# Moving the work of GpSimd, VectorE and ScalarE around an unchanged matmul sequence in a two-layer dense stage

## The chip, the cores and the metric

The kernel runs on one core of a Trainium2 chip. The metric is the device time of one execution in microseconds (us). Lower is better. The engines are named as in the profile: PE is TensorE (matmul; its weight loads are PEld), DVE is VectorE, ACT is ScalarE, POOL is GpSimd, SP is the engine that issues most of the DMAs.

## What is computed

Three layers follow each other: linear attention with random features, a mixture of experts (each token goes to one of eight), and a dense two-layer network with a piecewise quadratic gate. The change lies in the last one alone:

```python
def _moe2_ref(x, w_in, w_out) -> np.ndarray:      # x: 2304 x 512
    h = x @ w_in                                  # w_in: 512 x 2048
    beta = 1.0
    neg = h <= -beta
    pos = h >= beta
    g = np.where(pos, h, np.where(neg, 0.0, (h + beta) ** 2 / (4.0 * beta)))
    return (g @ w_out).astype(np.float32)         # w_out: 2048 x 512
```

The weights of this layer come as 64-bit floats, so the kernel first makes 32-bit ones of them.

## The kernel before

Precision: each product A x B runs as three matmuls of a fast 32-bit format, high x high, high x low and low x high. So every operand has a high part (ACT rounds it, `AF.Copy` into an F32R tile) and a low part (the operand less its high part, a subtraction of two SBUF tiles on POOL or DVE, here called a low).

The dense stage takes the hidden width of 2048 in four quarters `qd` of 512, and the 2304 tokens in six groups of G = 384.

**Quarter 0** (loop over `u` of 0 to 5) multiplies plainly. Per group PE runs `z_h(u,(0,1))`, `z_o(0,u-1,(2,3))`, `z_h(u,(2,3))`, `z_o(0,u,(0,1))`. A `z_h` call makes two 128-wide pieces of `h` (24 matmuls of 384 columns), a `z_o` call multiplies two pieces of `g` by `w_out` for three token tiles (18 matmuls of 512 columns). Group 0 lacks the second of the four.

**Quarters 1 to 3** make `h` by Winograd's form of Strassen's scheme, seven products in place of eight, in 18 calls `s_h(qd,p,a)` (three a quarter for p, two each for a). A call has seven products of six matmuls, added up in four PSUM banks b1 to b4; what goes from bank to bank goes through the SBUF tiles `tt`. After the first call comes one `z_o`, after each other call two (36 matmuls), and two more at the end.

The gate of one piece is a chain over two engines: `z_clip` clips on DVE (L1283) and squares on ACT (L1284), `z_g` takes a maximum on DVE (L1291), rounds on ACT (L1292) and makes the low (L1293), on the engine that is handed in.

What runs beside it, in pieces that `tick` and `beat` place in the program:

- `w_stream`: the weights. Of each 128x512 block of 64-bit numbers, `w_float32_steps` makes floats by one ACT and three DVE instructions (L252 to L257; a conversion). For quarters 1 to 3, sums of blocks of `w_in` (s1 to s4, on POOL, L337 to L351), then `op` rounds on ACT (L310) and `low` subtracts on POOL (L307).
- `y_stream`, in quarter 0 alone: 24 differences of blocks of x for the seven products (POOL, L1388), rounded on ACT (L1394), their lows on DVE (L1378), then stored to DRAM (`yd`, L1379 on SP). They go through four buffers `tt`; the fifth difference waits until the first is stored.
- `z_stream(u+1)`: high and low parts of x for the next group (`z_split`: ACT L1068, DVE L1069).
- `y_load` (POOL's DMA queue, L1415) fetches the stored differences again for the products, and results of a quarter are taken out of PSUM by ACT (L1342, tile `st` or `yW`) and added in DRAM by a DMA of POOL (L1352).

Each engine works through its own queue in program order; between engines there are only semaphores. So a step that a tick puts into ACT's queue stands ahead of everything that the program issues later on ACT, whether or not PE waits for that. `BEAT`, a string, says which stream goes on after every third (in `z_h`) or sixth (in `z_o`) matmul of quarter 0; `s_h` and `z_o` call `tick()` after each product or token tile, ahead of the eviction of that tile.

Of the kernel before, what the change touches and what calls it, by code (L numbers as in the profile page):

```python
# [19 lines left out]
P = 128  # L20
# [6 lines left out]
G = 384  # L27
# [134 lines left out]
def kernel(  # L162
# [131 lines left out]
    def w_stream():  # L294
        held = []

        def conv(t):
            key = wseq[wpos[1]]
            w_fetch()
            wpos[1] += 1  # L300
            low()
            yield from w_float32_steps(wraw.pop(key), t)

        def low():
            if held:
                hi, lo, t = held.pop()
                nc.gpsimd.tensor_sub(lo, t, hi.bitcast(F32))  # L307
# [9 lines left out]
        while wpos[1] < len(wseq) and wseq[wpos[1]][1] == 0:  # L317
            key = wseq[wpos[1]]
            t = wz[key[2] % 2]
            yield from conv(t)  # L320
            rnd(*w_new(key), t)
            yield
        for qd in range(1, 4):
            late = []
            for sub in range(2):
# [3 lines left out]
                if sub == 0:  # L329
                    while gate[1] < qd:  # L330
                        yield
# [7 lines left out]
                yield  # L339
                op(qd, 3, sub, a22)  # L340
                yield
                op(qd, 2, sub, a12)
                yield
                op(qd, 4, sub, s1)
                nc.gpsimd.tensor_sub(s2, s1, a11)
                yield
                op(qd, 1, sub, s2)
                nc.gpsimd.tensor_sub(s3, a22, s2)
                yield
                low()  # L350
                nc.gpsimd.tensor_sub(s4, a12, s2)  # L351
                yield
                late += [(qd, 5, sub, s3), (qd, 6, sub, s4)]
                if qd == 1:
                    for x in late:
                        op(*x)
                        yield
                    late = []
            n = (0, 1, 2, 3) if qd == 1 else (0, 3, 1, 2)
            yield from conv(wz[n[0]])  # L360
            yield from conv(wz[n[1]])
            while gate[0] < qd:
                low()
                yield
            for i in (5, 6):
                for x in late:
                    if x[1] == i:
                        op(*x)
                        yield
            for c in range(4):  # L370
                if c > 1:
                    yield from conv(wz[n[c]])
                rnd(*w_new(("wo", qd, c)), wz[n[c]])
                yield
            low()
            yield
# [688 lines left out]
    def z_split(u, d):  # L1065
# [3 lines left out]
        nc.vector.tensor_sub(yl, yT[d][:, c], yh.bitcast(F32))  # L1069
# [201 lines left out]
    streams = {"w": w_stream(), "y": None, "z": None}  # L1271

    def tick(name="w"):
        if streams[name] is not None:
            next(streams[name], None)
# [5 lines left out]
    def z_clip(ph):  # L1281
        cl = zp.tile([P, G], F32, name="cl", tag="cl", bufs=3)
# [4 lines left out]
    def z_g(ph, cl, key, eng):  # L1287
        qd, g, f = key
        gt = gs[g % 2][f + 4 * ((3 * qd + g // 2) % 2) if g % 2 and f < 2 else f]
        gh, gl = gt[:, 0], gt[:, 1]  # L1290
        nc.vector.tensor_tensor(out=cl, in0=ph, in1=cl, op=ALU.max)  # L1291
        nc.scalar.activation(gh, cl, AF.Copy)  # L1292
        eng.tensor_sub(gl, cl, gh.bitcast(F32))  # L1293
        gtiles[key] = (gh, gl)

    def z_h(u, fs):
        ph = {f: ps_h2.tile([P, 512], F32, name="ph2", tag="ph2")[:, 0:G] for f in fs}
        eng = [nc.gpsimd, nc.vector]
# [12 lines left out]
        todo = []  # L1311
        for f, d in order:
            mm(f, d)
            beat(u)
            if d == 3:
                todo.append((*z_clip(ph[f]), (0, u, f)))
                if len(todo) > 1:
                    z_g(*todo.pop(0), eng.pop(0))
        z_g(*todo.pop(0), eng.pop(0))

    def z_o(qd, g, fs):
        if fs[0] == 0:
            pos[qd, g] = [ps_o.tile([P, D], F32, name="po", tag="po") for _ in range(TG)]
        for j in range(TG):
# [3 lines left out]
            for f in fs:  # L1328
# [4 lines left out]
                nc.tensor.matmul(po, lhsT=gl[:, c], rhs=wh, start=False, stop=(f == 3))  # L1333
            if qd == 0:
                beat(5 if g == NG - 1 and fs[0] else g + fs[0] // 2)
            else:
                tick()
            if fs[0] == 0:
                continue
            st = z_stage(qd, g)[:, j * D:j * D + D]  # L1340
            if qd < 3:
                nc.scalar.activation(st, po, AF.Copy)  # L1342
            else:
                nc.vector.tensor_add(st, st, po)
                if t not in ends:
                    z_store(t, st)
# [279 lines left out]
```

## Time and profile before

| | us |
|---|---|
| median of 3 runs | 860.08 (860.07 to 864.66) |
| the profiled execution | 861.69 |
| its span, first to last instruction | 859.9 |
| PE busy in the span | 770.5 (90%) |
| DVE, ACT, POOL busy | 550.1, 404.6, 426.2 |
| granted clock of PE, mean of the span | 0.96 of full |

The dense stage lies between 393.56 us (its first matmul) and the end. In the slices of the page PE is busy nine tenths or more from 200 to 390 us, and has holes from 400 to 470 us and at some six places behind that. The granted clock (1.0 is 2.4 GHz, 0.5 is 1.2 GHz) is below full in those slices too. "<-" behind an idle time names what ended it.

### The profile page before, as it was taken

To read this page: it belongs to the slowest core of one execution; us is meant where nothing else is said; L and a number is where in the kernel's file an instruction comes from. 1 tells how busy PE (TensorE), PEld (TensorE's weight loads), DVE (VectorE), ACT (ScalarE), POOL (GpSimd) and SP (SyncE) were. 2 spreads that over 40 slices of the span, in tenths; PEclk is the share of its full clock that TensorE was granted. 3 is DMA by queue.
4 is the path that set the end of the run, shared out by engine and by line. 5 is a ranking of instruction groups with operands and counts; after the bars stand their busy time and mean duration, and the time that the engine had idled before them with its cause. 6 is when DMAs were issued, how large, how long until landed. Compare 5 with 4: busy or idle time off the path is not lost. (4 is left out here: it accounts for less than half of the span.)

```text
span 859.9 us, 17052 instructions
## 1 busy us (share of the span) xinstructions
PE 770.5 (90%) x6428; PEld 698.9 (81%) x6428; DVE 550.1 (64%) x1118; ACT 404.6 (47%) x991; POOL 426.2 (50%) x481
## 2 busy tenths in 40 slices
PE   6998899589999999998857999789979799799996
PEld 5887788389999999998645988678868789698984
DVE  4688888757566765569657656665576654646562
ACT  6998898144222222224355554554544444443330
POOL 5658832545556554356376434553435533433432
PEclk9999899799999999999978999989989899899999
DMA  9977101455667656534656477939696676858732
GB/s 212 220 190 207 35 29 52 128 189 181 211 194 224 201 179 203 172 123 147 215 219 239 195 276 263 352 100 327 179 276 206 199 248 144 280 139 314 293 112 78
DMA packets 94236, 166.61 MB, mean 194 GB/s; under 512 B 28528, under 2 KB 61424, under 8 KB 94144
## 3 DMA queue, kind: packets, MB, share of 16 engines
q1 hardware_dynamic: 79136, 93.91, 34.8%
q0 software_dynamic: 14112, 69.80, 25.4%
q10 hardware_dynamic: 896, 1.70, 0.6%
q8 instruction: 53, 0.87, 0.4%
q14 instruction: 39, 0.32, 0.1%
HBM read 125.29 MB, written 40.11 MB: 192 GB/s over the span
## 5 line engine op out<-in xcount | busy, mean ns | idle before, releaser
L1331 PE MATMUL po<-wh,g 128*128 128x512 f32 x288 | 117.1, 407 | 20.9 <-ACT st L1342 12.7
L278 POOL TENSOR_SCALAR wh<-wraw 128x1024 fp32r<-128x1024 f32 x60 | 75.0, 1251 | 102.0 <-DMA wraw<-in_moe_w_dram 71.3
L1284 ACT ACTIVATE cl<-cl,half 128x384 f32<-128x384 f32 x96 | 59.2, 617 | 134.5 <-DVE cl L1283 134.5
L1333 PE MATMUL po<-wh,g 128*128 128x512 f32 x288 | 117.3, 407 | 2.0 <-POOL g L1293 2.0
L1332 PE MATMUL po<-wl,g 128*128 128x512 f32 x288 | 116.6, 405 | 0.0
L1293 POOL TENSOR_TENSOR g<-cl,g 128x384 fp32r<-128x384 f32 x48 | 50.1, 1045 | 122.7 <-ACT g L1292 96.8
L381 DVE TENSOR_TENSOR wl<-wraw,wh 128x1024 fp32r<-128x1024 f32 x60 | 83.7, 1403 | 8.2 <-POOL wh L278 8.1
L607 ACT ACTIVATE pp<-ps,bi 128x128 f32<-128x128 f32 x288 | 85.2, 496 | 3.1 <-DVE bi L603 3.1
L1331 PEld LDWEIGHTS po<-wh,g 128*128 128x128 f32 x288 | 56.2, 195 | 34.7 <-ACT st L1342 13.3
L1147 PE MATMUL ph<-xh,wh 128*128 128x288 f32 (+6 forms) x256 | 76.8, 300 | 3.1 <-DVE hl L1153 2.5
L1165 PE MATMUL py<-hh,wh 128*128 128x288 f32 (+6 forms) x256 | 77.5, 303 | 0.0
L1148 PE MATMUL ph<-xl,wh 128*128 128x288 f32 (+6 forms) x256 | 76.6, 299 | 0.1
L1149 PE MATMUL ph<-xh,wl 128*128 128x288 f32 (+6 forms) x256 | 76.5, 299 | 0.0
L1167 PE MATMUL py<-hh,wl 128*128 128x288 f32 (+6 forms) x256 | 76.4, 299 | 0.0
L1166 PE MATMUL py<-hl,wh 128*128 128x288 f32 (+6 forms) x256 | 76.3, 298 | 0.0
L1333 PEld LDWEIGHTS po<-wh,g 128*128 128x128 f32 x288 | 56.0, 194 | 17.9 <-POOL g L1293 4.8
L1332 PEld LDWEIGHTS po<-wl,g 128*128 128x128 f32 x288 | 55.9, 194 | 12.2
L1292 ACT ACTIVATE g<-cl 128x384 fp32r<-128x384 f32 x96 | 49.9, 520 | 29.9 <-DVE cl L1291 29.8
L1427 PE MATMUL ph<-yS,wh 128*128 128x384 f32 x140 | 50.5, 361 | 14.0 <-ACT tt L1436 12.3
L1152 ACT ACTIVATE hh<-ph 128x288 fp32r<-128x288 f32 (+6 forms) x64 | 26.8, 418 | 72.8 <-PE ph L1149 70.3
L1153 DVE SCALAR_TENSOR_TENSOR hl<-ph,hh 128x288 fp32r<-128x288 f32 (+6 forms) x64 | 29.1, 461 | 49.6 <-ACT hh L1152 49.6
L596 DVE TENSOR_REDUCE nsq<-ps 128x4 f32<-128x512 f32 x72 | 46.9, 683 | 11.1 <-PE ps L591 10.9
(214 smaller groups left out, 2107.6 us busy)
## 6 DMA issues: line engine op xcount, KB each, us to landing
wraw<-in_moe_w_dram SPq DMA_DIRECT2D x57, 512.0 KB, 4.0
yS<-yd POOLq DMA_DIRECT2D x35, 768.0 KB, 11.1
ys<-yd POOLq DMA_DIRECT2D x28, 768.0 KB, 10.0
yd<-tt SPq DMA_DIRECT2D x24, 384.0 KB, 2.7
wraw<-in_moe_w_in_dram SPq DMA_DIRECT2D x16, 512.0 KB, 5.1
wraw<-in_moe_w_out_dram SPq DMA_DIRECT2D x16, 512.0 KB, 4.7
yd<-ys SPq DMA_DIRECT2D x9, 768.0 KB, 6.2
zd<-st SPq DMA_DIRECT2D x6, 768.0 KB, 4.1
```

The costliest lines, as they stand in the source:

```text
L278: nc.gpsimd.tensor_scalar(out=hi, in0=t, scalar1=1.0, scalar2=1.0, op0=ALU.mult, op1=ALU.mult)
L381: nc.vector.tensor_sub(lo, t, hi.bitcast(F32))
L607: act.activation(at(ppb)[:, 2 * j + i, :], at(pjb[i])[:, j, :], AF.Exp, bias=r["bi"][:, j, i:i + 1])
L1147: nc.tensor.matmul(ph, lhsT=wh[:, d, c], rhs=xh, start=(d == 0), stop=False)
L1148: nc.tensor.matmul(ph, lhsT=wh[:, d, c], rhs=xl, start=False, stop=False)
L1149: nc.tensor.matmul(ph, lhsT=wl[:, d, c], rhs=xh, start=False, stop=(d == 3))
L1165: nc.tensor.matmul(py, lhsT=wh[:, a, c], rhs=hh, start=(f == 0), stop=False)
L1166: nc.tensor.matmul(py, lhsT=wh[:, a, c], rhs=hl, start=False, stop=False)
L1167: nc.tensor.matmul(py, lhsT=wl[:, a, c], rhs=hh, start=False, stop=(f == 7))
L1331: nc.tensor.matmul(po, lhsT=gh[:, c], rhs=wh, start=(f == 0), stop=False)
L1332: nc.tensor.matmul(po, lhsT=gh[:, c], rhs=wl, start=False, stop=False)
L1333: nc.tensor.matmul(po, lhsT=gl[:, c], rhs=wh, start=False, stop=(f == 3))
```

## The change

PE's instruction sequence stays as it is, apart from which products the names 2 to 5 stand for. Everything else in the dense stage is dealt out anew:

- **Lows.** The gates' lows (`z_low`) all go to DVE; half of them were on POOL. POOL gets the lows of `z_split` (for the groups after the first) and those of `y_stream`; it keeps the weights' lows.
- **Sums.** The block sums of the weights (8 in a quarter) and the 24 differences of `y_stream` go from POOL to DVE.
- **Products.** In `s_h` the order of products is changed, so that after each of the first four one addition on DVE (with one operand in PSUM) follows, and each bank is written anew or added to only after that. The second copy on ACT (L1450) and the addition of two SBUF tiles (L1457) fall away.
- **Placing.** A stream now says of which kind its next step is ("D" has work on DVE, "A" none, "wait" is a gate), and a tick may ask for a kind. In `z_o` the ticks stand behind the eviction of the tile and only in the half with `fs = (2,3)`; in `s_h` two free ticks stand after the first two products, two for "A" later, none in the last three. In quarter 0 the beats go z, y, w, none, so that `y_stream` gets 6 steps in a group where it had 12.

```diff
         def conv(t):
+            yield "D"
             ...
-            yield from w_float32_steps(wraw.pop(key), t)
+            steps = w_float32_steps(wraw.pop(key), t)
+            next(steps)
+            yield "D"
+            next(steps)
...
-                s1, s2, s3, s4 = a21, a11, a22, a12
-                nc.gpsimd.tensor_add(s1, a21, a22)
+                s1, s2, s3, s4 = a21, a11, a21, a12
+                yield "D"
+                nc.vector.tensor_add(s1, a21, a22)
                 op(qd, 0, sub, a11)
-                yield
-                op(qd, 3, sub, a22)
+                yield "A"
+                op(qd, 3, sub, s1)
...
-    def z_split(u, d):
+    def z_split(u, d, eng=nc.vector):
         ...
-        nc.vector.tensor_sub(yl, yT[d][:, c], yh.bitcast(F32))
+        eng.tensor_sub(yl, yT[d][:, c], yh.bitcast(F32))
...
+    def tick(name, kinds="AD"):
+        s = streams.get(name)
+        if s and s[1] == "wait":
+            s[1] = next(s[0], None)
+        if s and s[1] and s[1] in kinds:
+            s[1] = next(s[0], None)
...
+    def z_low(gt, cl):
+        nc.vector.tensor_sub(gt[:, 1], cl, gt[:, 0].bitcast(F32))
...
     def z_o(qd, g, fs):
         ...
+            if fs[0]:
+                st = z_stage(qd, g)[:, j * D:j * D + D]
+                if qd < 3:
+                    nc.scalar.activation(st, po, AF.Copy)
+                ...
             if qd == 0:
                 beat(5 if g == NG - 1 and fs[0] else g + fs[0] // 2)
-            else:
-                tick()
+            elif fs[0]:
+                tick("w")
+                tick("w", "A")
...
     def y_stream():
-        def low():
+        def advance():
             if held:
                 p, op, s, hi, t, both = held.pop(0)
-                nc.vector.tensor_sub(t.bitcast(F32R), t, hi)
+                nc.gpsimd.tensor_sub(t.bitcast(F32R), t, hi)
                 nc.sync.dma_start(out=yd[p][op][:, s * 2 * G:(s + 1) * 2 * G], in_=both)
+            if high:
+                x = high.pop(0)
+                nc.scalar.activation(x[3].bitcast(F32R), x[4], AF.Copy)
+                held.append(x)
         ...
-                    nc.gpsimd.tensor_sub(t, x, y)
+                    nc.vector.tensor_sub(t, x, y)
...
-    BEAT = "zywzywzywzywyyywyyywyyyyyy"
+    BEAT = ("z", "y", "w", None)
     def beat(u):
-        tick(BEAT[count[u] % len(BEAT)])
+        n = count[u]
         count[u] += 1
+        if n < 16:
+            name = BEAT[n % 4]
+        else:
+            name = "yww"[(n - 16) % 3]
+        if name:
+            tick(name)
...
     def s_h(qd, p, a):
         product(0, b1, True)
-        nc.scalar.activation(s1, b1, AF.Copy)
+        nc.scalar.activation(x1, b1, AF.Copy)
+        tick("w")
         product(1, b2, True)
-        nc.vector.tensor_add(u2, b2, s1)
-        tick()
-        product(2, b1, False)
-        q11 = z_clip(b1)
-        tick()
-        ...
+        tick("w")
+        nc.vector.tensor_add(x1, x1, b2)
+        product(2, b3, True)
+        nc.vector.tensor_add(x2, x1, b3)
+        tick("w", "A")
+        product(3, b4, True)
+        nc.vector.tensor_add(x3, x2, b4)
+        tick("w", "A")
+        product(4, b1, False)
+        q11 = z_clip(b1)
+        product(5, b2, True)
+        nc.vector.tensor_sub(x2, x2, b2)
+        l11 = z_g(*q11, (qd, g0, f0))
+        q21 = z_clip(x2)
+        product(6, b4, False)
+        nc.vector.tensor_add(x1, x1, b4)
+        z_low(*l11)
+        ...
```

Three places of the program, engine by engine, show what is issued there. First ACT, in the second `z_o` ahead of the first call of `s_h` in quarter 2. L310 (L314 after) rounds weights, L252 starts a conversion, L1342 (L1361) takes a token tile out of PSUM, L1436 (L1468) copies the first product of the call. Before:

```order
L310 ACTIVATE wh5_3128<-yW_6744 128x512
L252 ACTIVATE wx_7717<-wraw_7332 128x512
L310 ACTIVATE wh6_3130<-wz1_3141 128x512
L252 ACTIVATE wx_7745<-wraw_7363 128x512
L1342 ACTIVATE yW_6744<-po_7705 128x512
L1342 ACTIVATE yW_6744<-po_7706 128x512
L310 ACTIVATE wh6_3130<-yW_6744 128x512
L1342 ACTIVATE yW_6744<-po_7707 128x512
L1436 ACTIVATE tt_7772<-ph2_7768 128x384
```

After:

```order
L1361 ACTIVATE yW_6752<-po_7674 128x512
L252 ACTIVATE wx_7704<-wraw_7432 128x512
L1361 ACTIVATE yW_6752<-po_7675 128x512
L314 ACTIVATE wh4_3126<-wz1_3141 128x256
L1361 ACTIVATE yW_6752<-po_7676 128x512
L314 ACTIVATE wh4_3126<-yW_6752 128x256
L314 ACTIVATE wh4_3126<-wz1_3141 128x256
L1468 ACTIVATE tt_7734<-ph2_7730 128x384
```

Ahead of the first eviction there stood four steps of the weights, two of them rounds that need a conversion just begun; now there is none.

Second DVE, in the same call of `s_h`. L253, L255 and L257 are a conversion, L1441, L1453 and L1455 (L1474 to L1488 after) the additions over banks, L1283 (L1304) a clip, L1291 (L1312) a maximum. Before:

```order
L1441 TENSOR_TENSOR tt_7772<-ph2_7769,tt_7772 128x384
L253 TENSOR_SCALAR wy_7792<-wraw_7714 128x512
L1283 TENSOR_SCALAR cl_7801<-ph2_7768 128x384
L255 SCALAR_TENSOR_TENSOR wy_7792<-wx_7791,wy_7792 128x512
L257 SCALAR_TENSOR_TENSOR wz0_3140<-wraw_7714,wy_7792 128x512
L1291 TENSOR_TENSOR cl_7801<-ph2_7768,cl_7801 128x384
L253 TENSOR_SCALAR wy_7818<-wraw_7742 128x512
L255 SCALAR_TENSOR_TENSOR wy_7818<-wx_7817,wy_7818 128x512
L257 SCALAR_TENSOR_TENSOR wz1_3141<-wraw_7742,wy_7818 128x512
L1453 TENSOR_TENSOR tt_7773<-ph2_7769,tt_7772 128x384
L1455 TENSOR_TENSOR tt_7772<-tt_7773,ph2_7770 128x384
```

After:

```order
L255 SCALAR_TENSOR_TENSOR wy_7705<-wx_7704,wy_7705 128x512
L257 SCALAR_TENSOR_TENSOR yW_6752<-wraw_7432,wy_7705 128x512
L1474 TENSOR_TENSOR tt_7734<-tt_7734,ph2_7731 128x384
L1476 TENSOR_TENSOR tt_7734<-tt_7734,ph2_7732 128x384
L1479 TENSOR_TENSOR tt_7735<-tt_7734,ph2_7733 128x384
L1304 TENSOR_SCALAR cl_7776<-ph2_7730 128x384
L1484 TENSOR_TENSOR tt_7734<-tt_7734,ph2_7731 128x384
L1312 TENSOR_TENSOR cl_7776<-ph2_7730,cl_7776 128x384
L1304 TENSOR_SCALAR cl_7788<-tt_7734 128x384
L1488 TENSOR_TENSOR tt_7734<-tt_7734,ph2_7733 128x384
L1317 TENSOR_TENSOR g00_5929<-cl_7776,g00_5929 128x384
```

The two conversions inside the call have gone; what remains of one stands ahead of the first addition, and a low (L1317) has come in.

Third POOL in quarter 0, in group 1. L1388 is a difference of `y_stream`, L1293 a gate's low, L337 a block sum, L307 (L300 after) a weight's low, L1402 a low of `y_stream`, L1077 a low of `z_split`. Before:

```order
L1388 TENSOR_TENSOR tt_6146<-tt_6121,yT_3145 128x384
L1388 TENSOR_TENSOR tt_6164<-yT_3145 128x384
L1293 TENSOR_TENSOR g10_5933<-cl_6137,g10_5933 128x384
L337 TENSOR_TENSOR wz0_3140<-wz0_3140,wz1_3141 128x2x128
L1388 TENSOR_TENSOR tt_6202<-yT3_3146,yT_3145 128x384
L307 TENSOR_TENSOR wl4_3127<-wz0_3140,wh4_3126 128x256
```

After:

```order
L1077 TENSOR_TENSOR ys0_3147<-yT_3145,ys0_3147 128x384
L1402 TENSOR_TENSOR tt_6101<-tt_6101 128x384
L300 TENSOR_TENSOR wl4_3127<-wz0_3140,wh4_3126 128x256
L1077 TENSOR_TENSOR ys0_3147<-yT3_3146,ys0_3147 128x384
L1402 TENSOR_TENSOR tt_6125<-tt_6125 128x384
L300 TENSOR_TENSOR wl5_3129<-wz0_3140,wh5_3128 128x256
```

POOL's instructions here are now lows alone, and they are of the same sizes as before.

## Rows read from the trace of the kernel before

**Rows 1.** Busy time by stretch: stretch, its us, each engine, PE's clock, DMA.

```profile
411.00:443.00 32.00, 21.84 (x84) 17.68 (x83) 20.05 (x30) 13.32 (x28) 16.08 (x16) 0.79 0.63 226
443.00:472.00 29.00, 19.68 (x87) 16.58 (x86) 19.58 (x29) 16.42 (x35) 21.74 (x21) 0.88 0.59 230
523.00:851.00 328.00, 299.83 (x1421) 265.21 (x1420) 195.26 (x341) 141.55 (x276) 140.45 (x175) 0.96 0.69 221
```

**Rows 2.** PE in time: start, us, line; first matmuls of parts, last one.

```profile
393.56 0.34 PE L1304 MATMUL ph<-ys,wh 128*128 128x384 f32 x1
...
410.91 0.34 PE L1304 MATMUL ph<-ys,wh 128*128 128x384 f32 x1
...
443.43 0.34 PE L1304 MATMUL ph<-ys,wh 128*128 128x384 f32 x1
...
472.18 0.34 PE L1304 MATMUL ph<-ys,wh 128*128 128x384 f32 x1
...
522.68 0.34 PE L1427 MATMUL ph<-yS,wh 128*128 128x384 f32 x1
...
692.30 0.34 PE L1427 MATMUL ph<-yS,wh 128*128 128x384 f32 x1
...
708.04 0.34 PE L1427 MATMUL ph<-ys,wh 128*128 128x384 f32 x1
...
851.07 0.40 PE L1333 MATMUL po<-wh,g 128*128 128x512 f32 x1
```

**Rows 3.** Waits of PE, 393 to 860 us: us in total, times, longest.

```profile
PE ph L1427 <- ACT tt L1436: 24.6, 6, 6.3
PE po L1331 <- ACT st L1342: 12.7, 2, 6.3
PE po L1331 <- ACT g L1292: 5.4, 2, 2.7
```

**Rows 4.** ACT in order of time, 558 to 560 us, with the idle time ahead.

```profile
558.16 0.42 ACT L310 ACTIVATE wh<-wz 128x256 fp32r<-128x256 f32 x1 [1.82 <-POOL wz L345]
558.48 1.06 ACT L1342 ACTIVATE yW<-po 128x512 f32<-128x512 f32 x2
559.44 0.49 ACT L1436 ACTIVATE tt<-ph 128x384 f32<-128x384 f32 x1
```

**Rows 5.** Waits of POOL and ACT, 393 to 472 us; a DMA's issues.

```profile
POOL tt L1388 <- DMA yd<-tt: 18.5, 8, 4.2
...
ACT tt L1394 <- POOL tt L1388: 26.0, 14, 3.4
...
yd<-tt SPq DMA_DIRECT2D x24, 384.0 KB, 2.7
```

**Rows 6.** Groups of instructions, 398 to 860 us: count, busy us, mean ns, idle before.

```profile
L1293 POOL TENSOR_TENSOR g<-cl,g 128x384 fp32r<-128x384 f32 x48 | 50.1, 1045 | 122.7 <-ACT g L1292 96.8 <-issue 19.3 <-PE ph L1429 3.4
L307 POOL TENSOR_TENSOR wl<-wz,wh 128x256 fp32r<-128x256 f32 x34 | 29.1, 856 | 2.7 <-ACT wh L310 2.6
...
L1293 DVE TENSOR_TENSOR g<-cl,g 128x384 fp32r<-128x384 f32 x48 | 31.4, 654 | 28.4 <-ACT g L1292 28.4
L255 DVE SCALAR_TENSOR_TENSOR wy<-wx,wy 128x512 int32<-128x512 int32 x25 | 21.9, 874 | 5.9 <-ACT wx L252 5.6
L1453 DVE TENSOR_TENSOR tt<-ph,tt 128x384 f32<-128x384 f32 x18 | 10.0, 556 | 19.7 <-PE ph L1429 19.7
```

**Rows 7.** DVE, then POOL, 530 to 535 us: start, us, instruction.

```profile
530.69 1.65 DVE L1457 TENSOR_TENSOR tt<-tt 128x384 f32<-128x384 f32 x1
533.58 0.55 DVE L1291 TENSOR_TENSOR cl<-tt,cl 128x384 f32<-128x384 f32 x1
...
530.51 1.41 POOL L307 TENSOR_TENSOR wl<-yW,wh 128x512 fp32r<-128x512 f32 x1
...
533.88 1.13 POOL L1293 TENSOR_TENSOR g<-cl,g 128x384 fp32r<-128x384 f32 x1 [1.95 <-ACT g L1292]
```

More of the change, by code (lines that the diff above doesn't have):

```diff
@@ L295, in w_stream, with low @@
         held = []
+        def low():
+            if held:
+                hi, lo, t = held.pop()
+                nc.gpsimd.tensor_sub(lo, t, hi.bitcast(F32))
         def conv(t):
+            yield "D"
             key = wseq[wpos[1]]
@@ L330, in w_stream @@
                     while gate[1] < qd:
-                        yield
+                        yield "wait"
                     for i in range(7):
@@ L1270, with stream, drain @@
     gs = [[zp.tile([P, 2, G], F32R, name=f"g{i}{f}", tag=f"g{i}{f}", bufs=1) for f in range(4 + 2 * i)] for i in range(2)]
[L1271 to L1275, printed above, removed]
+    streams = {}
+    def stream(name, steps):
+        streams[name] = [steps, next(steps, None)]
+    def tick(name, kinds="AD"):
[4 more added lines that the diff above has]
+            s[1] = next(s[0], None)
+    def drain(name):
+        while streams[name][1]:
+            tick(name)
+    stream("w", w_stream())
     def pair():
@@ L1279, in pair, with z_clip @@
         return t[:, 0:G], t[:, G:2 * G], t
-    def z_clip(ph):
-        cl = zp.tile([P, G], F32, name="cl", tag="cl", bufs=3)
+    def z_clip(ph, cl=None):
+        if cl is None:
+            cl = zp.tile([P, G], F32, name="cl", tag="cl", bufs=3)
         nc.vector.tensor_scalar(out=cl, in0=ph, scalar1=-1.0, scalar2=1.0, op0=ALU.max, op1=ALU.min)
@@ L1311, in z_h @@
         todo = []
+        lows = []
         for f, d in order:
@@ L1384, in y_stream @@
                 t1 = None
-                for op in (4, 5, 1, 3):
+                for op in (3, 2, 1, 5):
+                    yield "D"
                     hi, t, both = pair()
-                    x, y = {4: (b12, b11), 5: (b22, b12), 1: (b22, t1), 3: (t1, b21)}[op]
-                    nc.gpsimd.tensor_sub(t, x, y)
-                    if op in (4, 1):
+                    x, y = {3: (b12, b11), 2: (b22, b12), 1: (b22, t1), 5: (t1, b21)}[op]
+                    nc.vector.tensor_sub(t, x, y)
+                    if op in (3, 1):
                         t1 = t
-                    yield
-                    if len(held) > 1:
-                        low()
-                    nc.scalar.activation(hi.bitcast(F32R), t, AF.Copy)
-                    held.append((p, op, s, hi, t, both))
-        while held:
-            yield
-            low()
+                    advance()
+                    high.append((p, op, s, hi, t, both))
+        while high or held:
+            yield "A"
+            advance()
     def z_stream(u):
         for d in range(4):
-            z_split(u, d)
-            yield
-    BEAT = "zywzywzywzywyyywyyywyyyyyy"
+            yield "A"
+            z_split(u, d, nc.gpsimd)
+    BEAT = ("z", "y", "w", None)
     count = [0] * NG
     def beat(u):
-        tick(BEAT[count[u] % len(BEAT)])
+        n = count[u]
         count[u] += 1
+        if n < 16:
+            name = BEAT[n % 4]
+        else:
+            name = "yww"[(n - 16) % 3]
+        if name:
+            tick(name)
     def y_load(k):
@@ L1419, in s_h @@
         k0 = 7 * (3 * (qd - 1) + p)
-        b1, b2, b4, b3 = [ps_h2.tile([P, 512], F32, name="ph2", tag="ph2")[:, 0:G] for _ in range(4)]
+        b1, b2, b3, b4 = [ps_h2.tile([P, 512], F32, name="ph2", tag="ph2")[:, 0:G] for _ in range(4)]
         def product(i, bank, first):
@@ L1475 @@
             gate[0] = 1
[L1476 to L1477 removed]
+        drain("z")
         if u == NG - 2:
[L1479 to L1481 removed]
+            drain("y")
             y_slots()
```

120 lines of the change are left out of this document (48 added, 72 removed).

## The prediction

> **What bounds the kernel now.** I first looked where PE stands still, since the change leaves PE's own sequence alone. In the stretches by engine [rows 1] PE is busy 21.84 of 32 us and 19.68 of 29 us in the middle of quarter 0, and 299.83 of 328 us in quarters 1 to 3, and its granted clock there is 0.79, 0.88 and 0.96 of full. So time goes twice: PE waits, and after a long wait it runs at 1.2 GHz for a while.
>
> The first matmuls of the parts give the size of both together [rows 2]. Groups 3 to 5 of quarter 0 take from 472.18 to 522.68 us, 16.83 us a group, without a hole; group 0 lacks a quarter of that and should take 12.6. Quarter 0 should then take 12.6 + 5 x 16.83 = 96.8 us. It takes 522.68 - 393.56 = 129.1, so 32.3 are lost: 17.35 - 12.6 = 4.7 in group 0 (to 410.91), 32.52 - 16.83 = 15.7 in group 1 (to 443.43), 28.75 - 16.83 = 11.9 in group 2 (to 472.18). Behind it, a call of `s_h` with two `z_o` takes 708.04 - 692.30 = 15.74 us where nothing waits. Eighteen of these and half a pair of `z_o` more (4.2, a quarter of 16.83) make 287.5. From 522.68 to the end of the last matmul (851.07 + 0.40) it is 328.8, so 41.3 us are lost. Together 73.6 us.
>
> Who is waited for stands in PE's waits [rows 3]: nearly all is ACT, in short copies. L1436 (24.6 us, six times) is the copy of the first product of `s_h`, and PE may not add to that bank before it; L1342 (12.7 us, twice) takes `po` out. Neither is slow, 0.49 and about 0.53 us [rows 4]. They stand behind a round of weights that itself waited 1.82 us for POOL's block sum (L345), as ACT's queue shows [rows 4]. In quarter 0 the head of the queue is another: POOL's differences (L1388) wait 18.5 us in all for the store of a `tt` buffer, and ACT's rounds of them wait 26.0 us for POOL [rows 5], with the squares and evictions behind them. So the bound is the order in ACT's queue, fed by a slow chain through POOL, and not the sum of any engine's work: DVE has 195.26 us and POOL 140.45 in 328 [rows 1].
>
> **What the change does to quarters 1 to 3.** What goes: the four weight steps ahead of the first eviction, POOL's block sums from the chain, conversions inside `s_h`, and two instructions a call (L1450, L1457). What comes to DVE there: two lows a call in place of POOL's, 0.65 us each for 1.05 [rows 6], and the 24 block sums. Their price on DVE has no row: at most the 0.65 of a low of 384 columns [rows 6], at least nothing; I take 0.4, near two thirds of the low, since they have 256 columns. In sum DVE gains 36 x 0.65 + 24 x 0.4 - 18 x 0.55 (L1457, priced as its like [rows 6]) = 23 us in 328, beside 195 busy [rows 1], so it stays under 70% and I cost it at nothing; the cover is its idle third. It would cost only where DVE is late for PE.
>
> Three deadlines say where that could be. A product takes (15.74 - 8.4) / 7 = 1.05 us. Product 4 adds to b1, 3.15 us after the end of product 0, and ACT's copy has at most a weight round or two ahead of it: safe. Product 5 overwrites b2, so L1474 has 3.15 us from the end of product 1; ahead of it are at most two steps of up to two conversion instructions, 4 x 0.87 = 3.5 us [rows 6], begun at or before the end of the last `z_o`, 2.1 us ahead: some 1.7 us to spare. The third is at the end of a call with a = 1. The next-but-one `z_o` half needs the low of piece f = 3 after 4.2 us and five matmuls more of 4.2 / 18 = 0.23 us, so 5.4 us after product 6. DVE has six instructions up to that low, 6 x 0.56 = 3.3 us, and ACT's square and round between them, about 0.5 us each [rows 4]: done at 4.3, 1.1 us to spare. A low of POOL met on the way (0.86) leaves 0.3. I charge the nine such calls 0.5 us each, 4.5 us in all. The ends are nothing, and 18 calls with 0.86 + 0.56 (one POOL low, one DVE instruction), 26 us.
>
> **Quarter 0.** The 24 differences are spread over four groups and a bit, six a group for twelve. The `tt` buffer of a difference is stored two steps later and needed again two steps after that, and two steps are at least one `z_o` half, about 4.2 us, against a low of 1.05 and a store of 2.7 us [rows 5, 6]: it fits, on average with room (16.83 / 3 = 5.6), and a late store now holds DVE, not POOL. What I see late next is the SBUF access that DVE and POOL share. An addition of two SBUF tiles on DVE took 1.65 us while POOL was in a low from 530.51 to 531.92; it ended at 532.34, 0.42 after it. And POOL's low of 533.88, begun inside a DVE maximum that ended at 534.13, took 1.13 and so began its 1.0 us of work at about 534.0 [rows 7]. So of the two only one works at a time, DVE for about 0.42 us of its 0.55. Additions with an operand in PSUM keep their 0.556 [rows 6]. That makes a sum for each group, scaled by columns to 0.28 for a block sum and 0.56 for a conversion instruction. A group has 4 lows of `z_split` and 6 of `y_stream` on POOL, 10 x 1.05 = 10.5, and 4 gates' lows and 6 differences on DVE, 10 x 0.42 = 4.2.
> Group 1: 4 weights' lows (3.4), 2 conversion instructions (1.1), 3 block sums (0.8): 20.0, over 16.83 by 3.2.
> Group 2: 3 lows (2.6), two conversions (3.4), 1 sum (0.3): 21.0, over by 4.2.
> Group 3: 4 lows (3.4), 3 sums (0.8): 18.9, over by 2.1.
> Group 4 has three differences' lows and one difference left and stays under. Group 0 begins with the backlog of the stage before, as now, and I leave its 4.7. Quarter 0 then loses 14.2 us for 32.3. Its ends: 4.7 if the two engines' work falls between each other, and twice 14.2 if every block also holds DVE's clips up and the clock falls.
>
> The Trainium skill (page SBUF — State Buffer, section Who interferes with whom) says of this pair that whoever starts first holds it for the whole instruction. By that rule, with 0.55 in place of 0.42, the groups would be over by 5.2, 6.5 and 3.7, and the time would be an estimated 6 us longer, 811. The trace here has 0.42 behind POOL's end, so I stay with the row.
>
> **The sum.** Lost now 73.6; lost after 14.2 + 4.5 = 18.7; gain 54.9. The profiled execution had 861.69 us, which would become 806.8; the median of the runs is 1.6 lower, 860.08, and becomes **805**.
>
> **The rivals.**
> *The shared access bites harder.* DVE's queue is in order, so a blocked low also holds clips and maxima that need no such access, and POOL's lows often stand two or three in a row. For it speaks 1.65 us in place of 0.55 [rows 7]; against it, that PE has 8 us between a `z_h` and the `z_o` that uses it. Losses of 28 in quarter 0 and 4 to 8 behind: 73.6 - 34 = 40 gained, 820.
> *PE waits for DVE in every call.* If the 1.7 and 0.3 us to spare are not there, PE stops at product 5 or in `z_o` each time: 26 us behind quarter 0 and 14 to 18 in it, 830. If some stops also pull the clock down, up to 845. For it: DVE is now the only engine in each chain. Against it: 195 of 328 us busy, and the five additions of a call all have an operand in PSUM.
> *The change doesn't do it.* Queues stay in order; if the weight rounds still wait for DVE's tail of a call, ACT's evictions are late as before, and of the 18 us that quarter 0 gains the shared access may take half: 851 to 858. Against it: ahead of the first eviction there is no weight step left.
> *Slower.* The differences sit on DVE now, and each waits for the landing of a store. Eight waits of POOL took 18.5 us, 2.3 each, the longest 4.2 [rows 5]. If all 24 held DVE so long that PE lost 2.3 us each, that were 55 us, and the time would be as now (805 + 55 = 860). It is slower from 2.7 us each (870), and 906 with 4.2. Against it: half as many differences a group.
>
> **Chances.** The forecast (796 to 813) 0.58, harder access (813 to 826) 0.17, waits for DVE (826 to 848) 0.10, no effect (848 to 866) 0.07, slower (over 868) 0.08. The range holds 8 in 10 with the first two and some of the third: 794 to 830; 794 is the sum with quarter 0 at its lower end (805 - 9.5) and a little. A measurement of this kernel can tell about 1% from no change; by that, faster 0.86, same 0.06, slower 0.08.
>
> **What would show it.** Right: in the trace after, PE's waits name ACT's copy and eviction lines for a few us at most; the calls of `s_h` with their `z_o` take 15.7 to 16.5 us throughout, at full clock; groups 1 to 3 of quarter 0 take 19 to 21 us, with DVE's two-SBUF-tile instructions well over 0.55 us there. Wrong: groups 1 to 3 at 16.8 (the sharing costs nothing, and I am too high), a wait of DVE for `yd<-tt` of over 10 us, or waits of PE at product 5 or 6, which would be DVE's additions L1474 and L1479.

## The result, and the profile of the changed kernel

The changed kernel takes 811.14 us (median of 4 runs, 809.15 to 813.82), the kernel before beside it 861.12 (860.07 to 864.66). The ratio is 0.9415, with an interval of 0.9374 to 0.9455: faster by 5.9%. The forecast was 805, with a range of 794 to 830.

The profiled execution took 813.82 us, with a span of 812.0. PE is busy 756.6 us of it (93%), DVE 551.7 (68%), ACT 393.4 (48%), POOL 380.1 (47%), at a granted clock of 0.978.

The first matmuls of the groups of quarter 0, the first of `s_h` and the last matmul of all answer to [rows 2]. They are rows of PE in order of time: start, us, line.

```profile
396.27 0.34 PE L1326 MATMUL ph<-ys,wh 128*128 128x384 f32 x1
...
412.77 0.34 PE L1326 MATMUL ph<-ys,wh 128*128 128x384 f32 x1
...
431.21 0.34 PE L1326 MATMUL ph<-ys,wh 128*128 128x384 f32 x1
...
453.23 0.34 PE L1326 MATMUL ph<-ys,wh 128*128 128x384 f32 x1
...
476.87 0.34 PE L1326 MATMUL ph<-ys,wh 128*128 128x384 f32 x1
...
494.27 0.34 PE L1326 MATMUL ph<-ys,wh 128*128 128x384 f32 x1
...
511.29 0.34 PE L1459 MATMUL ph<-yS,wh 128*128 128x384 f32 x1
...
802.18 0.39 PE L1357 MATMUL po<-wh,g 128*128 128x512 f32 x1
```

Quarter 0 takes 511.29 - 396.27 = 115.0 us, 18.2 over its 96.8. By group it is over by 3.9, 1.6, 5.2, 6.8, 0.6 and 0.2 (the ideal is 12.6 for group 0 and 16.83 for each other). Quarters 1 to 3 take 802.57 - 511.29 = 291.3 us, 3.8 over their 287.5. Before it was 32.3 and 41.3. The gain in the dense stage is thus 14.1 + 37.5 = 51.6 us. Of this 3.7 are not seen in the total: the stage begins 2.7 us later (396.27 for 393.56), though what lies ahead of it is the same code, and behind the last matmul there are 9.4 us where there were 8.4. In the kernels below the same stage begins anywhere from 391.4 to 399.9 us, so that is spread from run to run.

The stretches of groups 2 and 3 and of quarters 1 to 3 [as in rows 1]: stretch, its us, the engines, PE's clock, DMA share, GB/s.

```profile
431.00:453.00 22.00, 19.07 (x86) 16.15 (x84) 12.92 (x22) 11.72 (x27) 16.55 (x18) 0.92 0.61 242
453.00:477.00 24.00, 19.79 (x87) 16.41 (x86) 17.60 (x27) 11.18 (x25) 14.41 (x14) 0.93 0.57 216
...
512.00:803.00 291.00, 288.44 (x1419) 257.76 (x1418) 194.60 (x393) 130.75 (x257) 91.55 (x125) 0.99 0.77 254
```

In quarters 1 to 3 PE is busy 288.4 of 291 us. DVE has 52 instructions more than before in those quarters (393 for 341) and still no more busy time, 194.60 us for 195.26.

What is left of waiting in quarter 0 (waits from 396 to 512 us: us in total, times, longest) answers to [rows 3, 5]:

```profile
ACT cl L1305 <- DVE cl L1304: 31.2, 13, 5.5
POOL ys L1077 <- ACT ys L1076: 26.4, 9, 6.2
...
DVE tt L1417 <- DMA yd<-tt: 11.1, 4, 3.8
...
PE po L1355 <- ACT st L1361: 6.7, 4, 2.7
```

PE's wait for ACT's eviction is half of what it was, and the wait for the store of a `tt` buffer has gone from POOL (18.5 us) to DVE (11.1 us). Around 450 us these lines form a ring. DVE, ACT and POOL in order of time, with the idle time ahead in brackets:

```profile
452.67 0.60 DVE L1417 TENSOR_TENSOR tt<-tt,yT 128x384 f32<-128x384 f32 x1 [3.83 <-DMA yd<-tt]
453.19 1.23 DVE L253 TENSOR_SCALAR wy<-wraw 128x512 int32<-128x512 int32 x1
454.53 1.04 DVE L255 SCALAR_TENSOR_TENSOR wy<-wx,wy 128x512 int32<-128x512 int32 x1
455.61 1.39 DVE L257 SCALAR_TENSOR_TENSOR wz<-wraw,wy 128x512 int32<-128x512 int32 x1
456.92 0.54 DVE L1304 TENSOR_SCALAR cl<-ph 128x384 f32<-128x384 f32 x1
...
457.56 0.61 ACT L1305 ACTIVATE cl<-cl,half 128x384 f32<-128x384 f32 x1 [5.52 <-DVE cl L1304]
...
447.82 1.43 POOL L1077 TENSOR_TENSOR ys<-yT,ys 128x384 fp32r<-128x384 f32 x1 [2.62 <-ACT ys L1076]
449.21 1.01 POOL L1402 TENSOR_TENSOR tt<-tt 128x384 fp32r<-128x384 f32 x1
...
454.98 1.47 POOL L1402 TENSOR_TENSOR tt<-tt 128x384 fp32r<-128x384 f32 x1
461.66 1.02 POOL L1077 TENSOR_TENSOR ys<-yT,ys 128x384 fp32r<-128x384 f32 x1 [5.21 <-ACT ys L1076]
```

DVE's difference (452.67) waits until a store has landed. The store follows a low on POOL (449.21), which stood behind a low that waited for a round of ACT (447.82). While DVE waits, the next clip (456.92) waits behind it in DVE's queue, and so it does for a conversion, 3.8 us long, that stands between the two (453.19 to 457.00). ACT's square (457.56) waits 5.52 us for that clip, and ACT's next rounds wait behind the square, for which POOL waits again (461.66).

The 6.8 us of group 3 show another order. There ACT's square waits for a clip that stands behind a second conversion (DVE, 461.18 to 464.66; two of its instructions, L255 and L257, take 1.53 and 1.32 us, where each takes 0.69 alone), with no wait for a store between. PE then waits for an eviction behind that gate's rounds:

```profile
465.96 0.62 ACT L1305 ACTIVATE cl<-cl,half 128x384 f32<-128x384 f32 x1 [3.66 <-DVE cl L1304]
```

```profile
471.02 0.50 PE L1355 MATMUL po<-wh,g 128*128 128x512 f32 x1 [2.67 <-ACT st L1361]
```

The 3.8 us of quarters 1 to 3 all lie in the first call of `s_h` and the half `z_o` behind it. PE's row and POOL's rows there:

```profile
518.22 0.42 PE L1459 MATMUL ph<-ys,wh 128*128 128x384 f32 x1 [1.54 <-DMA ys<-yd]
...
511.20 1.47 POOL L300 TENSOR_TENSOR wl<-wz,wh 128x512 fp32r<-128x512 f32 x1 [12.79 <-ACT wh L314]
512.62 1.63 POOL L1447 DMA_DIRECT2D ys<-yd  x3
```

Product 5 waits 1.54 us for its loaded operand (then 0.6 for DVE), and 3.4 us at half the clock follow from 520.3. Each other call of `s_h` takes 7.31 to 7.37 us and each pair of `z_o` 8.36 to 8.40.

### The profile page after: what moved, and what is told of

The parts are those of the page before. It is cut to its first block, busy times and chain, and to the rows that moved or that the text cites. A ratio compares the mean times of both kernels' runs of the same rounds, so it can differ in the third digit from the quotient of the medians.

```text
span 812.0 us, 17047 instructions
## 1 busy us (share of the span) xinstructions
PE 756.6 (93%) x6428; PEld 689.6 (85%) x6428; DVE 551.7 (68%) x1170; ACT 393.4 (48%) x973; POOL 380.1 (47%) x429
## 5 line engine op out<-in xcount | busy, mean ns | idle before, releaser
L1305 ACT ACTIVATE cl<-cl,half 128x384 f32<-128x384 f32 x78 | 47.3, 609 | 88.1 <-DVE cl L1304 88.0
L300 POOL TENSOR_TENSOR wl<-wz,wh 128x256 fp32r<-128x256 f32 (+1 forms) x43 | 40.2, 939 | 90.6 <-ACT wh L314 90.3
L1317 DVE TENSOR_TENSOR g<-cl,g 128x384 fp32r<-128x384 f32 x78 | 44.0, 565 | 23.5 <-ACT g L1313 23.5
L1313 ACT ACTIVATE g<-cl 128x384 fp32r<-128x384 f32 x78 | 40.5, 519 | 29.0 <-DVE cl L1312 28.8
```

## The experiments

All times stand beside runs of the kernel before on the same chip (its medians there 860.32 to 863.56). The last two columns are the loss of one profiled execution, reckoned as above. Kernels whose code of quarters 1 to 3 is that of the change lose 1.4 to 3.8 us there, so a difference of 2 us in one profile tells nothing. The profiled execution of h1 took 826.64 us, 4.8 above its median, that of the changed kernel 2.7 above its own.

| kernel | median us | ratio to before | lost in quarter 0 | lost in 1 to 3 |
|---|---|---|---|---|
| before | 860.08 | | 32.3 | 41.3 |
| changed | 811.14 | 0.9415 (0.9374 to 0.9455) | 18.2 | 3.8 |
| e1_b_place | 859.75 | 0.9972 (0.9944 to 1.0) | 32.5 | 38.8 |
| e2_a_ahead | 811.79 | 0.9416 (0.9383 to 0.945) | 18.1 | 1.9 |
| e3_a_sums | 812.03 | 0.9402 (0.936 to 0.9444) | 18.7 | 2.7 |
| e4_a_lows | 808.69 | 0.9383 (0.9349 to 0.9417) | 18.1 | 2.0 |
| f1_store1 | 803.75 | 0.9342 (0.9315 to 0.9369) | 12.9 | 1.6 |
| f2_zdve | 814.90 | 0.9472 (0.9443 to 0.9502) | 23.3 | 1.4 |
| f3_yl | 811.72 | 0.9433 (0.9406 to 0.9459) | 18.1 | 2.1 |
| f4_both | 803.24 | 0.9322 (0.9294 to 0.935) | 12.7 | 0.3 |
| g1_b_order | 852.02 | 0.9891 (0.9857 to 0.9924) | 32.1 | 31.8 |
| g2_a_place6 | 816.00 | 0.9471 (0.9428 to 0.9513) | 18.0 | 7.4 |
| g3_a_all3 | 809.74 | 0.9397 (0.9358 to 0.9436) | 18.7 | 4.2 |
| h1_a_places | 821.88 | 0.9502 (0.9459 to 0.9545) | 18.1 | 18.0 |

### Quarters 1 to 3: one edit at a time

e1 takes the kernel before and puts the weight steps of `z_o` behind the eviction, e2 puts them ahead of it again in the changed kernel:

```diff
+            if qd and fs[0]:
+                tick("w")
+                tick("w", "A")
             if fs[0]:
                 st = z_stage(qd, g)[:, j * D:j * D + D]
...
-            elif fs[0]:
-                tick("w")
-                tick("w", "A")
```

> The kernel before with one edit: in z_o of quarters 1 to 3 the tick stands behind the eviction of the token tile, not ahead of it. Engines, products and all other ticks are as before. Theory of the queue (what PE lost there was the place of weight steps ahead of ACT's evictions and of the copy of the first product): of the 41 us lost in quarters 1 to 3 at least 20 come back, so 840 us or less. Rival, the engines (block sums and half of the lows on POOL made the steps late): under 5 us come back, 855 or more.

> The changed kernel with the two ticks of z_o in quarters 1 to 3 put back ahead of the eviction. Theory of the queue: 20 to 40 us are lost again in quarters 1 to 3, 831 to 851 us, and PE waits for ACT's lines of eviction and copy. Rival, the engines: under 5 us, 811 to 816, since sums and lows are on DVE.

e3 gives the block sums back to GpSimd, e4 the lows of the first two gates of a call:

```diff
-                nc.vector.tensor_add(s1, a21, a22)
+                nc.gpsimd.tensor_add(s1, a21, a22)
...
-        z_low(*l11)
+        z_low(*l11, nc.gpsimd)
```

> The changed kernel with the block sums of the weights back on POOL. Theory of the queue: the sums are not what PE waited for; under 4 us either way, 808 to 815. Rival, the engines: half of the gain of quarters 1 to 3 goes, 825 or more.

> The changed kernel with two of the four gates' lows of a call in quarters 1 to 3 back on POOL (those of the first token group of the pair, as before). Theory of the queue: the low that z_o needs after a call with a = 1 comes about 0.6 us later than on DVE, with 1.1 us to spare by the prediction: under 5 us, 811 to 816. Rival, the engines: 10 us or more, 821 or more.

None of the four moves the time by 1%. The place behind the eviction alone is worth nothing to the kernel before, and undoing it, or either move off GpSimd, costs the changed kernel nothing. So neither the theory that a step ahead of the eviction was the cause nor the theory that slow GpSimd work was the cause can stand by itself. It remained that any one of the three is enough, or that the gain lies in what all these kernels share: the order of products, and the number and kind of steps. Three kernels tell this apart. g3 is the changed kernel with the edits of e2, e3 and e4 in one. g2 changes only the places in `s_h`:

```diff
         nc.vector.tensor_add(x3, x2, b4)
-        tick("w", "A")
+        tick("w")
         product(4, b1, False)
         q11 = z_clip(b1)
+        tick("w")
         product(5, b2, True)
```

and g1 is the kernel before with the new order of products and banks, and with it the new additions (the second copy on ACT and the addition of two SBUF tiles fall away there too):

```diff
-        product(2, b1, False)
-        q11 = z_clip(b1)
+        product(2, b3, True)
+        nc.vector.tensor_add(x2, x1, b3)
         tick()
         product(3, b4, True)
+        nc.vector.tensor_add(x3, x2, b4)
         tick()
+        product(4, b1, False)
+        q11 = z_clip(b1)
```

> The kernel before with one thing of the change: the seven products' numbering and order, and the banks and sums of s_h that go with it. The matmul that starts on a bank that ScalarE must first have copied out is then that of product 4, three products (3.1 us) after product 0, where it was product 2, one product after; no other bank is read before it is used again in the call, and the conversion of the weights, its steps, their five or six places, the GpSimd block sums and lows stay those of before. If the time of quarters 1 to 3 went to that one short deadline (theory of the order): their loss falls from 41 us to under 12, and the time from 860 to 825-835. If it went to the weight steps standing among the products (theory of the places): 850-862. If it needs the order and one of the three GpSimd edits together: 840-850.

> The changed kernel with the weight steps in s_h at the six places of the kernel before (after products 0 to 4 and behind the last piece, each taking a step of either engine), instead of four of which the last two take ScalarE's steps only. Theory of the order: the deadlines keep their slack, quarters 1 to 3 lose under 4 us, 809-815. Theory of the places: the steps stand before the clips again, each late clip holds the next product, quarters 1 to 3 lose 15 us or more, 825 or over.

> The changed kernel with the three edits that did nothing alone undone together: weight steps ahead of the eviction in the output product, the block sums on GpSimd, and the lows of the first two gates on GpSimd. If any one of the three was enough (theory of redundancy): with none left the loss of quarters 1 to 3 comes back by 15 us or more, 825 or over. If none is needed beside the order of the products and the steps' kinds: 808-816.

g3 is as fast as the changed kernel: GpSimd's share of this work is not what the gain comes from. The stretch of its quarters 1 to 3, to be read beside that of the changed kernel above:

```profile
512.00:803.00 291.00, 288.66 (x1421) 257.95 (x1419) 201.84 (x340) 132.06 (x257) 146.80 (x177) 0.99 0.77 255
```

POOL works 55 us longer there, and PE loses nothing by it. g2 fits neither of its two theories: it loses 7.4 us in quarters 1 to 3, between the under 4 of the one and the 15 of the other.

g1 gains 1.1%, and its loss in quarters 1 to 3 falls by 9.5 us of 41.3. Its 852 us lie in the range of the theory of the places, and the theory that the short deadline was all of it falls too. PE still waits for the same copy, though three products lie between it and its use now. PE's wait from 390 us on, and ACT's queue where one of them ends (the copy is L1436):

```profile
PE ph L1427 <- ACT tt L1436: 15.9, 6, 3.8
```

```profile
629.60 0.66 ACT L252 ACTIVATE wx<-wraw 128x512 f32<-128x512 f32 x1
630.17 1.05 ACT L1342 ACTIVATE yW<-po 128x512 f32<-128x512 f32 x2
632.42 0.63 ACT L310 ACTIVATE wh<-yW 128x512 fp32r<-128x512 f32 x1 [1.20 <-DVE yW L257]
632.96 0.58 ACT L1342 ACTIVATE yW<-po 128x512 f32<-128x512 f32 x1
633.44 0.48 ACT L1436 ACTIVATE tt<-ph 128x384 f32<-128x384 f32 x1
```

The copy stands behind an eviction, the eviction behind a round of weights, and the round waits for the conversion on DVE that was begun one tick earlier, one conversion after the other. Before, a unit of `s_h` and two `z_o` had twelve places for such steps by the program, six in `s_h` and six in the two `z_o` (the expectation of h1 counts ten). The changed kernel has ten, and five of them take ACT's steps alone. I took their number and places for the rest of the cause. h1 therefore gives the changed kernel all the places of before, with steps of any kind:

```diff
+            if qd:
+                tick("w")
             if fs[0]:
                 st = z_stage(qd, g)[:, j * D:j * D + D]
...
-            elif fs[0]:
-                tick("w")
-                tick("w", "A")
```

(and `s_h` as in g2).

> The changed kernel with every place of a weight step in quarters 1 to 3 as in the kernel before: six in s_h, and one in each of the four tiles of a pair of output products, ahead of the eviction, each taking the next step of either engine (before: ten a unit; the changed kernel takes at most two of any kind and two of ScalarE's in s_h, and in the output product none in the first two tiles of a group, two in each of the last two). The order of the products, the contents of the steps, the block sums and lows on VectorE stay those of the change. Theory that the order of the products (41.3 us of loss to 31.8 alone) and the metering of the steps together made the gain: conversions pile up on VectorE and roundings on ScalarE in front of the copy of product 0 again, quarters 1 to 3 lose 20 us or more, 828-845. Theory that the rest came from what a step holds (a block sum and its rounding in steps apart, lows behind the next piece): they lose 4 to 10 us, 811-819.

It lies between the two theories' figures: 821.88 us, and in the profiled execution 14.2 us of loss come back. By the ratios (0.9502 for 0.9415) it is 7.5 us, so the profiled execution gives too much. PE's waits from 390 us on, and ACT's queue ahead of one of them:

```profile
PE ph L1458 <- DVE tt L1478: 4.7, 3, 2.4
PE ph L1458 <- ACT tt L1467: 4.5, 2, 2.2
```

```profile
614.04 0.63 ACT L314 ACTIVATE wh<-yW 128x512 fp32r<-128x512 f32 x1 [1.22 <-DVE yW L257]
614.58 0.58 ACT L1363 ACTIVATE yW<-po 128x512 f32<-128x512 f32 x1
615.05 0.48 ACT L1467 ACTIVATE tt<-ph 128x384 f32<-128x384 f32 x1
```

This is the row pattern of g1 again. So the 37.5 us of quarters 1 to 3 split along one path, by the profiles: 9.5 with the order of products (41.3 to 31.8, g1), 13.8 between g1 and h1 (31.8 to 18.0), and 14.2 with the places and kinds of the steps (18.0 to 3.8). By the ratios, less the 14 us that quarter 0 gives between g1 and h1, it is 9.4, 19.5 and 7.5, each good to some 5 us. Of the last, the places in `s_h` alone are 3.6 in the profile (g2), 5 by the ratios. What is between g1 and h1 are the contents of the steps, the engines of sums and lows, and how far quarter 0 has brought the stream. At the new places the engines are worth nothing (g3); at the old ones they were not tried alone. How this part divides, the largest by the ratios, stays open.

### Quarter 0: shared access or the ring of buffers

The prediction put the loss of groups 1 to 3 down to the SBUF access that DVE and POOL share. The rival, from the rows around 450 us, is the ring through the four `tt` buffers. f1 makes the low and the store of a difference one step earlier (the low overwrites the difference, so those who read it must go ahead, and the order of the four changes):

```diff
-            if held:
-                p, op, s, hi, t, both = held.pop(0)
-                nc.gpsimd.tensor_sub(t.bitcast(F32R), t, hi)
-                nc.sync.dma_start(...)
             if high:
-                x = high.pop(0)
-                nc.scalar.activation(x[3].bitcast(F32R), x[4], AF.Copy)
-                held.append(x)
+                p, op, s, hi, t, both = high.pop(0)
+                nc.scalar.activation(hi.bitcast(F32R), t, AF.Copy)
+                nc.gpsimd.tensor_sub(t.bitcast(F32R), t, hi)
+                nc.sync.dma_start(...)
...
-                for op in (3, 2, 1, 5):
+                for op in (3, 1, 5, 2):
```

f2 takes the 20 lows of `z_split` off POOL, and with them some of the collisions (`z_split(u, d)` in `z_stream`, the engine of before):

> The changed kernel with y_stream's round, low and store all in the step after the difference (the store one step sooner), for which its operations go in the order 3, 1, 5, 2. Theory of the ring (in quarter 0 a difference on DVE waits for a store that stands behind POOL's low, which stands behind ACT, which stands behind DVE): DVE's waits for yd<-tt fall from 11.1 us to under 3, and quarter 0 loses 8 to 11 us in place of 18; 801 to 804 us. Rival, the shared access as the prediction has it: quarter 0 still loses 16 or more, 809 to 813.

> The changed kernel with the lows of z_split back on DVE (20 instructions of 0.42 us of access there for 20 of 1.05 on POOL). Theory of the shared access: each of groups 1 to 3 holds 2.5 us less of it, quarter 0 loses 11 to 13 in place of 18, 804 to 807 us. Theory of the ring: the waits for yd<-tt stay or grow, since DVE gets more to do: 809 to 815.

Against the changed kernel f1 gains 6 to 7 us, as the ring has it, though quarter 0 still loses 12.9 where 8 to 11 were expected. f2 loses 4 to 5 (its interval just touches that of the changed kernel, but its quarter 0 loses 5.1 us more). Its time is the one that the theory of the ring gave, but not by that theory's sign: DVE's waits for `yd<-tt` were to stay or grow, and f2 has none. In their place DVE waits 12.1 us for ACT's rounds of the very lows that the edit puts into its queue. So f2 shows that fewer collisions alone do not help here, and it does not show the ring. In f1's waits (393 to 503 us) there is no wait of DVE for a store any more, and POOL's for ACT's rounds is half; in f2's (396 to 517 us) PE's wait for evictions is nearly double that of the changed kernel, and DVE waits for the rounds that POOL had waited for. First f1, then f2:

```profile
POOL ys L1077 <- ACT ys L1076: 12.8, 6, 4.9
...
PE po L1355 <- ACT st L1361: 6.1, 3, 2.8
```

```profile
PE po L1355 <- ACT st L1361: 12.4, 4, 4.7
...
DVE ys L1077 <- ACT ys L1076: 12.1, 14, 1.1
```

The sharing itself is real in all of them. I added up by how much DVE's instructions on SBUF alone took longer than their like with POOL idle (0.55 us for 384 columns, 0.41 for a block sum, 0.43 and 0.69 for a conversion's): 17.5 us in quarter 0 of before, 18.0 in the changed kernel, 20.8 in f1, 14.3 in f2. The losses are 32.3, 18.2, 12.9 and 23.3. f1 has the most of the collisions and the least loss, so their sum does not set the loss.

By group f1 loses 2.9, 3.0, 1.0, 6.0 and twice nothing, where the changed kernel lost 3.9, 1.6, 5.2, 6.8, 0.6 and 0.2. What the ring cost is thus seen in group 2 (DVE's waits of 2.9 and 1.5 us for a store, at 432.1 and 441.5, lie there; PE's clock is 0.92 in it, 1.00 in f1), and hardly in the rows around 450 us. The largest loss, that of group 3, stays without any wait for a store. The two waits shown above for that group are there in f1 too, behind a conversion again (453.55 to 457.01):

```profile
458.32 0.62 ACT L1305 ACTIVATE cl<-cl,half 128x384 f32<-128x384 f32 x1 [3.62 <-DVE cl L1304]
```

```profile
463.38 0.50 PE L1355 MATMUL po<-wh,g 128*128 128x512 f32 x1 [2.68 <-ACT st L1361]
```

### The first call of `s_h`

I took the wait at 518.22 for a place in POOL's queue: the load of product 5 is issued at 512.62, behind a low that waited 12.79 us. f3 issues it, and the next, with the first five:

```diff
-            for k in range(5):
+            for k in range(7):
                 y_load(k)
```

> The changed kernel with the loads of differences 5 and 6 issued at the end of group 4, with those of 0 to 4, and not behind POOL's low of the first output weights. If the wait of PE for ys<-yd in the first call of s_h came from POOL's queue: that call takes 7.4 to 8.2 us in place of 10.7, 807 to 809 us in all. If it came from the transfers' own length: it stays over 10, 810 to 812.

> f1 and f3 together: by the theory of the ring and of POOL's queue the two gains add up, 797 to 802 us; by their rivals it stays at 808 or more.

In f3 they are issued at 501.83, 13 us ahead of the quarter's first product (514.79) where it was 1.3 us behind it, and PE waits as before. POOL's row, PE's wait (512 to 530 us), the DMA's share in 40 slices of the same 18 us, and the two loads' size and median time to landing:

```profile
501.83 1.12 POOL L1447 DMA_DIRECT2D ys<-yd  x2
```

```profile
PE ph L1459 <- DMA ys<-yd: 1.4, 1, 1.4
```

```profile
DMA  9999999999999999999999999999999998210000
```

```profile
ys<-yd POOLq DMA_DIRECT2D x2, 768.0 KB, 20.3
```

In the changed kernel the loads issued from 512.62 on landed after a median of 6.8 us. In these 18 us the DMA engines are full until about 527 us, and in f3 an earlier issue lands no earlier: 6.6 and 8.5 us after the quarter's first product, 6.8 and 8.7 in the changed kernel. So POOL's queue was not the cause there.

f4, with f1 and f3 together, has the lowest median of all, 803.24 us, 6.8% less than before (797 to 802 were expected); from f1 (803.75) it can't be told by these intervals. Both are faster than the changed kernel. In its trace, though, the early issue does help. The loads land 2.7 and 5.5 us after the quarter's first product, 5.8 and 8.0 in f1, PE waits for none, and quarters 1 to 3 lose 0.3 us. f1 still has this:

```profile
PE ph L1456 <- DMA ys<-yd: 0.8, 1, 0.8
```

The landing of the load before them tells the two cases apart. In the changed kernel it lands 4.0 us into the quarter, when the next was issued at 1.3: an earlier issue only waits longer. In f1 it lands at 1.05, before the next is issued at 1.35, and there an earlier issue gains. No run tests this further.

## Why the prediction was right, and where it was not

**The sum.** The profiled execution was to take 806.8 us and took 813.82, 7.0 more: 4.0 in quarter 0 (18.2 for 14.2), 0.7 less behind it (3.8 for 4.5), 2.7 of a later start and 1.0 of a longer end, which no step of the prediction spoke of. The size of the two stages' gain, 51.6 us for 54.9, is right.

**What bounds the kernel** was read rightly: PE waited for short instructions of ACT, behind others in its queue. PE's waits for those lines in quarters 1 to 3 are gone. But the reading of what held ACT's queue was one row, a round that waited for POOL's block sum [rows 4], and it was not typical of what mattered: with the sums on POOL again (e3, g3) nothing is lost. Rounds that wait for a conversion begun a tick before held it as well (g1, h1). In the kernel before, they waited longer than those for that sum (523 to 852 us):

```profile
ACT wh L310 <- DVE wz L257: 6.4, 3, 2.4
ACT wh L310 <- POOL wz L345: 6.0, 3, 2.2
ACT wh L310 <- DVE yW L257: 3.2, 3, 1.2
```

What frees the queue is in part the longer way from copy to use (g1) and in part fewer places, half of them for ACT's steps alone (h1). The part between them, 13.8 us in the profiles, has no shown cause. The prediction named these parts in one breath and gave none a size; e1 shows that the one it put first, the step ahead of the eviction, is worth nothing alone.

**DVE's burden.** The lows and sums were to add 23 us to DVE's 195. It has 194.60. The step priced each at its own duration and left out that POOL's instructions, which stretch those of DVE [rows 7], go away with them. With them back on POOL, g3, DVE has 53 instructions fewer and 7 us more. Reckoned as above for quarter 0, DVE's instructions on SBUF alone were lengthened in quarters 1 to 3 by some 21 us before, 4 in the changed kernel and 33 in g3. The price of a block sum, 0.4 us by estimate, is 0.41 to 0.42 with POOL idle, and 0.95 to 1.23 beside a low of POOL.

**The three deadlines** hold. The calls with a = 1 were charged 0.5 us each and lost nothing; the 3.8 us lost lie in the first call, by a load, which the prediction had not looked at. The sum of 4.5 was near for the wrong reason. The sign it gave for failing, PE waiting at the additions of products 5 and 6, came in h1 (L1478, product 6: 4.7 us), with a conversion ahead of the addition.

**Quarter 0** was mis-sized, and its mechanism was at best a part; that its total came within 4 us owes something to errors that cancel. By group the forecast was 4.7, 3.2, 4.2, 2.1 and nothing behind; measured are 3.9, 1.6, 5.2, 6.8, 0.6 and 0.2. None of groups 1 to 3 took the 19 to 21 us that were to show it right (18.4, 22.0, 23.6). Two steps failed. One is the place of the conversions: the sum has two in group 2 and none in group 3, and in the trace none runs in group 2 and two in group 3 (453.19 and 461.18), each ahead of a clip for which ACT waits; the sum, moreover, counts work and no such waiting. The other is the sentence that the ring of four buffers fits "on average with room". It reckoned a low and a store against the time of two steps, and left out that the low waits in POOL's queue behind rounds of ACT, which wait behind squares, which wait for clips behind the very difference. The sign that the prediction gave against itself, a wait of DVE for the store of over 10 us, came: 11.1 us. So the mechanism of its slower rival was at work, in four places of 24, and without it quarter 0 loses 5 us less (18.2 to 12.9 in f1, which changes the order of the four differences too). What the other 12.9 us are, sharing or conversions ahead of clips, was not separated; in group 3 both are at work, a conversion that POOL's lows stretch. By the whole-instruction rule of the Trainium skill (SBUF — State Buffer, Who interferes with whom; the section words it for two-port modes of VectorE, and of an instruction with two SBUF inputs it says that it contends) the time came out at an estimated 811, which is what was measured, but by 5.2, 6.5 and 3.7 us in groups 1 to 3, and not as it fell: that they agree in the sum is luck. The conversion instruction L257 at 455.61 met a low of POOL (454.98) and ended 0.55 us after it, with 0.69 of its own: near the rule, a little under it.

## What to carry to other kernels

Where a short copy is late, look at how much slack the consumer leaves and where work is fed into the copy's queue, before looking at which engine does the feeding: here the engines could be exchanged freely once the rest of the change was in. A ring of buffers that goes through several in-order queues has to be reckoned with everything that stands ahead in each of them; here starting its last leg one step earlier took its waits away. When several edits come together, undo them one at a time and also all at once: single reversals that cost nothing said here only that the cause lay elsewhere.

## What was not expected of the hardware

Giving VectorE GpSimd's instructions left its busy time where it was: 393 instructions in 194.60 us against 340 in 201.84 (g3). The instructions that met one of GpSimd had been the longer ones, as above in quarter 0. And loads issued 14 us earlier landed no earlier while those ahead of them were still under way: their time to landing went from a median of 6.8 us (three loads) to 20.3 (two). In f4, where the loads ahead were through sooner, the same early issue brought them 2.5 to 3.2 us forward against f1.
